# First batch's strided pairs: queries and keys as 2 KB rows, transposed by pairs of neighbouring tokens

## The chip, the cores and the metric

The kernel runs on one core of a Trainium2 chip. The metric is the device time of one execution in microseconds (us). Engines are named as in the profile: PE (TensorE) multiplies matrices, PEld is its weight load, DVE (VectorE), ACT (ScalarE) and POOL (GpSimd) work on vectors, SP (SyncE) issues transfers (DMAs). A few transfers of the start are issued by ACT.

## The reference

Attention over 8 batches, 8 heads, 576 tokens of 64 numbers, then a two-layer network over all 4608 tokens. The first four heads attend to the last 32 tokens ("local"), the last four to the earlier tokens whose number is the same modulo 32 ("strided").

```python
stride = 32
scores = scale * np.matmul(q, k.transpose(0, 1, 3, 2))
rel = pos[:, None] - pos[None, :]
mask_local = (rel >= 0) & (rel < stride)
mask_strided = (rel >= 0) & (pos[None, :] % stride == pos[:, None] % stride)
...
x = np.ascontiguousarray(attn_out.transpose(0, 2, 1, 3)).reshape(B * S, H * D)
h = x @ w_in            # 512 x 2048
g = h * np.clip(h + 3.0, 0.0, 6.0) / 6.0
return (g @ w_out).astype(np.float32)
```

The two weight matrices come as 64-bit floats. Queries, keys and values are 32-bit.

## The kernel before

**Heads by pairs.** Two heads of a batch, 2 x 64 rows, make a pair, four pairs a batch. In batch 0 pairs 0 and 1 are local, pairs 2 and 3 strided. `kept_pair(g)` lays out the work of one pair. For batch 0 (`early` is not 0):

- `load` (L488 to L491) brings queries (tile `qn`) and keys (`kn`) with eight successive tokens on each of 72 partitions. For each token and head this is a run of 64 numbers, 256 bytes, so one load has 72 x 8 x 2 = 1152 runs. It is issued as two DMAs, 64 partitions and 8.
- `tr` (L494 to L498) turns them by eight matmuls with the identity, one for each of the eight token places, into two PSUM banks (`qp`, `kp`): 128 rows (two heads of 64), 72 columns for each place. `evac` (L500 to L512) copies the banks into the layout that the scores read (`qplain`, `kplain`, and for strided pairs `qt`, `kt`).
- `scores` (L593 to L609) writes the mask by a matmul and adds queries by keys to it (`ps`, two banks). A local pair has 36 small matmuls, a strided one 64.
- Then the softmax: maximum and sum on DVE (`st`), subtraction and scaling on POOL (`e`, L636 to L668), exponential on ACT. Local pairs are turned back by PE (`turned`, `pt`, L725), strided ones by DVE (L702, L713, tiles `at`, `atkept`).
- `both` (L746) and `both_mm` (L766 to L772) multiply by the values (`pv`), and `keep_x` splits the result into a rounded part on ACT (L430) and a rest on DVE (L433): `x_00`, `x_01` for pair 0, up to `x_30`, `x_31`.

**Network.** `ffn(0)` multiplies these x tiles by the first weights (`ph`, L921 to L923: three matmuls for each chunk of 128 channels), in the order of `TURNS`: pair 0, 2, 1, 3. `gate_of` forms the gate on ACT (L956) and DVE (L960, tile `u`), then come the second weights (`acc`, L854 to L856).

**Weights.** `weight_part` loads each 128 x 512 block of 64-bit floats (`rawi`, `rawo`, L303, 512 KB) and turns it into two 32-bit tiles: two ACT passes, a DVE join (L319), a rounded part on ACT or POOL, a rest on POOL or DVE (L337).

**Order.** Nothing is issued in the order in which it is written. Each step is an `op` with an engine, a cost in us, the tiles that it reads and writes, and a due time. `Plan.emit` plays all steps through by these costs and writes the instructions of every engine in the order that comes out. A changed cost or due time can therefore move instructions everywhere in the program. `emit` also puts idle matmuls (`idle`, L1254) where it sees PE waiting early on. Each engine runs its own row in order, and waits at an instruction until its inputs are there.

Of the kernel before, what the change touches and what calls it, by code (L numbers as in the profile page):

```python
# [20 lines left out]
P = 128  # L21
# [4 lines left out]
NQB = 6  # L26
# [8 lines left out]
FIRST = (-57.0, -53.9, -56.5, -53.8)  # L35
QK = (-60.0, -59.0, -55.0, -52.0)
VAL = (-56.0, -53.0, -51.0, -49.0)
# [18 lines left out]
HOP = 0.12  # L56

WARM = 100.0
IDLE = 0.43
FETCH = 2.6  # L60
WORDS = 256
# [4 lines left out]
class Plan:  # L66
# [29 lines left out]
    def emit(self, idle):  # L96
# [6 lines left out]
        ready = {e: [] for o in ops for e in o[0]}  # L103
        free = dict.fromkeys(ready, 0.0)
        avail = [o[9] for o in ops]
# [81 lines left out]
def attention_ffn(ctx: ExitStack, tc, q, k, v, w_in, w_out, out):  # L187
# [252 lines left out]
    def kept_pair(g):  # L440
# [37 lines left out]
        for x in "qk":  # L478
# [6 lines left out]
            if early:  # L485

                def load(x=x, nkey=nkey):
                    t = new(wp, nkey, [P, RUN, 2, D], F32, f"{x}n{nm}")  # L488
                    rows = {"q": q, "k": k}[x][b, h0:h0 + 2].rearrange("j (p i) d -> p i j d", i=RUN)
                    for part in (slice(0, D), slice(D, S // RUN)):  # L490
                        (nc.scalar if g < 2 and x == "k" else nc.sync).dma_start(t[part], rows[part])  # L491
                tb = [slot(early) for _ in range(2)]

                def tr(x=x, nkey=nkey, tb=tb):  # L494
                    n = S // RUN
                    ps = [psum(tb[h], f"{x}p{nm}{h}") for h in range(2)]
                    for i in range(RUN):
                        nc.tensor.transpose(ps[i // 4][:, i % 4 * n:i % 4 * n + n], tiles[nkey][:n, i].rearrange("p j d -> p (j d)"), tiles["ident",][:n, :n])  # L498

                def evac(e, x=x, tb=tb, h=0):  # L500
                    ps, to, half = tiles[tb[h].key][:, :S // 2], qk_of(x), slice(RUN // 2 * h, RUN // 2 * h + RUN // 2)
                    if loc:
                        c0 = PAD if x == "k" else 0
                        to = to[:, c0:c0 + S].rearrange("c (p i) -> c p i", i=RUN)[:, :, half]
                        ps = ps.rearrange("c (i p) -> c p i", i=RUN // 2)
                    else:
                        to = to.rearrange("c (t a m) -> c t a m", t=RUN, a=4)[:, half, :, :NPOS]
                        ps = ps.rearrange("c (t m a) -> c t a m", t=RUN // 2, a=4)
                    if e == "ACT":
                        nc.scalar.copy(to, ps)  # L510
                    else:
                        nc.vector.tensor_copy(to, ps)  # L512
                op("ACT" if g < 2 and x == "k" else "SP", 1.7, load, writes=[nkey], due=QK[g] + 0.1 * (x == "k") - 900 * (g < 2 and x == "k"), after=1.7)
                op("PE", 0.7 * slow, tr, words=2 * RUN, reads=[("ident",), nkey, "plain", tkey[x]], writes=tb, take=tb, due=due - 1020, mode="s")
                for h in range(2):
                    op({"ACT": 0.45, "DVE": 0.4} if loc else {"ACT": 0.65, "DVE": 0.65}, 0, partial(evac, h=h), reads=[tb[h]],
                       writes=[tkey[x]] if h == 0 else [tkey[x] + (1,) if isinstance(tkey[x], tuple) else tkey[x] + "1"], give=tb[h], due=due - 19)
                continue
# [22 lines left out]
        def load_v():  # L541
# [14 lines left out]
            for a in range(4):  # L556
                nc.sync.dma_start(tiles[vkey][PAD * a:PAD * a + NPOS].rearrange("p j t d -> p j (t d)"), rows[a])
        op("SP", 3.9 if shifted else 1.5, load_v, writes=[vkey, skey] if shifted else [vkey], due=VAL[g] if early else due - 30, early=0 if early else due - 35, after=3.6 if shifted else 2.0)

# [54 lines left out]
        def keep(e, j):  # L614
# [8 lines left out]
        sd = due - 12  # L623
        op("PE", ((2.0 if loc else 1.75) if early else 1.5) * slow, scores, reads=["const", qkey, kkey, *both_halves], writes=[*sb, ekey, ekey + "1", stkey],
           take=sb, due=sd - 1000, room=0.0 if early else ROOM, mode="s", words=4 * 2 * (18 if loc else 32) + 6)
# [91 lines left out]
        if shifted:  # L717
# [16 lines left out]
            def both():  # L734
                ps, at, vt = [psum(vb[h], f"pv{nm}{h}") for h in range(2)], tiles[akey], tiles[vkey]
                half = 3 * NQB // 2
                for h in range(2):
                    for x in range(half):
                        for j in (h, 1 - h):
# [6 lines left out]
                            nc.tensor.matmul(ps[bank][own, PAD * x:PAD * x + PAD], vu, at[own, n0:n0 + PAD], start=True, stop=True)  # L746
            op("PE", 0.72 * slow, turned, reads=[("ident",), ekey, ekey + "1"], writes=[*tb, akey, akey + ("b",)], take=tb, due=due - 1002, mode="s", words=4 * NQB)
            for h in range(2):
# [16 lines left out]
        else:  # L765
            def both_mm():  # L766
                ps, vt = [psum(vb[h], f"pv{nm}{h}") for h in range(2)], tiles[vkey]
                for i in range(8):
                    for j in range(2):
                        at = tiles["at1", i // 4][:, i % 4] if akeys[j] == "at1" else tiles[akeys[j]][:, i]  # L770
                        nc.tensor.matmul(ps[i // 4][D * j:D * j + D, i % 4 * P:i % 4 * P + 4 * NPOS], vt[:, j, i],
                                         at.rearrange("p (a m) -> p a m", a=4)[:, :, :NPOS], start=True, stop=True)  # L772
# [515 lines left out]
```

## Time and profile before

| | |
|---|---|
| median of 3 runs | 928.04 us (926.23 to 931.61) |
| profiled execution | 929.12 us |
| its span, first to last instruction | 927.3 us |
| PE busy over the span | 885.3 us, 95% |
| DVE / ACT / POOL busy | 53% / 44% / 46% |
| mean granted PE clock | 0.978 |

The span is that of the profiled execution; its time is 1.8 us more. The busy shares are means over the whole program, in which attention of a batch and the network of others alternate, and say little of the first tenth, where batch 0 has to be loaded and attended before the network can start. The views by window and in order of time show that part by itself. In them a row has its start, its length, the engine and line, the tiles, and in brackets the idle time ahead of it with what ended it.

### The profile page before, as it was taken

How to read it: one execution, taken by the hardware profiler on the slowest of the kernel's cores; microseconds unless marked ns; L12 is line 12 of the kernel's file. 1: busy time of each engine (PE TensorE's matmuls, PEld its weight loads, DVE VectorE, ACT ScalarE, POOL GpSimd, SP SyncE). 2: the span in 40 equal slices, each digit the busy share in tenths (PEclk: the TensorE clock that was granted, in tenths of full speed). 3: DMA queues.
4: the chain of work that ended last, by engine and by line, in shares of the span. 5: the costliest groups of instructions: out<-in, count | busy, mean ns of one | idle time of the engine just before them, and what ended most of it. 6: DMA issues, size and time to landing. Idle time of an engine off the chain costs nothing.

```text
span 927.3 us, 19470 instructions
## 1 busy us (share of the span) xinstructions
PE 885.3 (95%) x7747; PEld 711.9 (77%) x7747; DVE 488.8 (53%) x833; ACT 404.6 (44%) x736; POOL 428.6 (46%) x378
## 2 busy tenths in 40 slices
PE   5789898999999999999999999999999999999997
PEld 3668686776888788888788778888887887888786
DVE  3788866568766777466755723345457003323200
ACT  2656655333434435344444633444446234334421
POOL 3646765555765877222221955213139531112441
PEclk7579999999999999999999999999999999999999
DMA  9988999977688874799784687785745675555374
GB/s 161 236 251 206 249 236 333 282 177 190 181 197 242 209 189 112 205 260 230 218 209 149 194 257 196 238 210 192 227 156 211 200 236 185 194 192 188 120 213 137
DMA packets 229563, 191.71 MB, mean 207 GB/s; under 512 B 174944, under 2 KB 189280, under 8 KB 229472
## 3 DMA queue, kind: packets, MB, share of 16 engines
q1 hardware_dynamic: 226800, 189.35, 73.2%
q10 hardware_dynamic: 2672, 1.11, 0.6%
q8 instruction: 61, 1.00, 0.5%
q14 instruction: 30, 0.25, 0.1%
HBM read 157.91 MB, written 32.51 MB: 205 GB/s over the span
## 4 chain that ended last, share of the span: by engine, by line
PE 75%; POOL 6%; DMA 6%; DVE 5%; SPq 3%; issue 2%; ACT 2%; DVEq 0%; POOLq 0%; ACTq 0%
PE ph L1094 8%; PE ph L1095 7%; PE ph L1096 7%; PE acc L854 4%; PE acc L856 4%; PE acc L855 4%; PE ph L921 3%; PE ph L922 3%; PE ph L923 3%; PE ps L608 3%; DMA rawi<-in_moe_w_in_dram 3%; DMA qn<-in_q_dram 2%; POOL xc L1033 2%; PE acc2b L854 2%; PE acc2b L856 2%
## 5 line engine op out<-in xcount | busy, mean ns | idle before, releaser
L1113 DVE TENSOR_TENSOR htmp<-ph,htmp 128x512 f32<-128x512 f32 x72 | 49.7, 690 | 183.9 <-ACT htmp L1105 106.7
L1094 PE MATMUL ph<-xc,wi 128*128 128x512 f32 x336 | 133.4, 397 | 1.3 <-DVE htmp L1113 0.8
L1095 PE MATMUL ph<-xc,wi 128*128 128x512 f32 x336 | 131.1, 390 | 0.0
L1096 PE MATMUL ph<-xc,wi 128*128 128x512 f32 x336 | 130.9, 390 | 0.0
L890 POOL TENSOR_TENSOR g<-u,g 128x512 fp32r<-128x512 f32 x48 | 65.7, 1372 | 62.1 <-ACT g L887 50.1
L921 PE MATMUL ph<-x,wi 128*128 128x512 f32 x192 | 79.8, 415 | 7.9 <-DVE u L960 4.6
L922 PE MATMUL ph<-x,wi 128*128 128x512 f32 x192 | 76.8, 400 | 4.0 <-DVE x L433 2.6
L923 PE MATMUL ph<-x,wi 128*128 128x512 f32 x192 | 76.7, 399 | 0.8 <-POOL wi L337 0.8
L854 PE MATMUL acc<-wo,g 128*128 128x512 f32 x192 | 76.9, 401 | 0.0
L855 PE MATMUL acc<-wo,g 128*128 128x512 f32 x192 | 75.1, 391 | 1.5 <-issue 1.1
L1094 PEld LDWEIGHTS ph<-xc,wi 128*128 128x128 f32 x336 | 63.0, 188 | 17.2 <-DVE htmp L1113 2.0
L856 PE MATMUL acc<-wo,g 128*128 128x512 f32 x192 | 75.4, 392 | 0.2 <-POOL g L890 0.2
L1096 PEld LDWEIGHTS ph<-xc,wi 128*128 128x128 f32 x336 | 63.1, 188 | 13.4
L1095 PEld LDWEIGHTS ph<-xc,wi 128*128 128x128 f32 x336 | 63.1, 188 | 12.4
L708 DVE STREAM_TRANSPOSE atloc<-e 32x192 f32<-32x192 f32 x168 | 61.9, 369 | 15.9 <-POOL e L668 9.0
L1105 ACT COPY htmp<-ph 128x512 f32<-128x512 f32 x72 | 42.2, 587 | 50.0 <-PE ph L1096 48.1
L653 POOL TENSOR_TENSOR e<-e,st 128x288 f32<-128x288 f32 (+1 forms) x30 | 34.2, 1141 | 64.5 <-DVE st L631 64.4
L890 POOL TENSOR_TENSOR g12a<-u,g02a 128x512 fp32r<-128x512 f32 x16 | 20.6, 1289 | 83.4 <-ACT g02a L887 83.4
L956 ACT ACTIVATE u<-htmp,three 128x512 f32<-128x512 f32 x48 | 34.7, 723 | 44.5 <-DVE htmp L1113 44.5
L956 ACT ACTIVATE u<-ph,three 128x512 f32<-128x512 f32 x48 | 33.0, 688 | 44.2 <-PE ph L923 43.8
L960 DVE SCALAR_TENSOR_TENSOR u<-u,htmp 128x512 f32<-128x512 f32 x48 | 38.5, 802 | 22.9 <-ACT u L956 22.8
L890 POOL TENSOR_TENSOR g11a<-u,g01a 128x512 fp32r<-128x512 f32 x16 | 21.5, 1347 | 60.4 <-ACT g01a L887 52.2
(212 smaller groups left out, 2079.5 us busy)
## 6 DMA issues: line engine op xcount, KB each, us to landing
wo<-wod SPq DMA_DIRECT2D x128, 512.0 KB
wi<-wid SPq DMA_DIRECT2D x84, 512.0 KB
rawi<-in_moe_w_in_dram SPq DMA_DIRECT2D x16, 512.0 KB
rawo<-in_moe_w_out_dram SPq DMA_DIRECT2D x16, 512.0 KB
wod<-wo SPq DMA_DIRECT2D x16, 512.0 KB
wid<-st SPq DMA_DIRECT2D x64, 128.0 KB
qn<-in_q_dram SPq DMA_DIRECT2D x112, 72.0 KB
kn<-in_k_dram SPq DMA_DIRECT2D x112, 72.0 KB
```

Of the source, the lines that this page charges most:

```text
L708: nc.vector.transpose(at[PAD * (a + h):PAD * (a + h) + PAD, :, PAD * a:PAD * a + PAD], e[PAD * a:PAD * a + PAD, :, PAD * h:PAD * h + PAD])
L854: nc.tensor.matmul(acc, gh, woh, start=fc == 0, stop=False)
L855: nc.tensor.matmul(acc, gh, wol, start=False, stop=False)
L856: nc.tensor.matmul(acc, gl, woh, start=False, stop=end)
L890: on(e).tensor_tensor(out=to(1), in0=tiles[uk], in1=tiles[gk[0]].bitcast(F32), op=ALU.subtract)
L921: nc.tensor.matmul(ph, wih, xh, start=n_ == 0, stop=False)
L922: nc.tensor.matmul(ph, wih, xl, start=False, stop=False)
L923: nc.tensor.matmul(ph, wil, xh, start=False, stop=n_ == NCC - 1)
L956: nc.scalar.activation(make(), src(), AF.Relu, bias=three)
L1094: nc.tensor.matmul(ph, w[:, j, 0], x[:, 0], start=u in (0, 1, 3) and j == 0, stop=False, skip_group_check=u in (2, 4, 5, 6))
L1095: nc.tensor.matmul(ph, w[:, j, 0], x[:, 1], start=False, stop=False, skip_group_check=u in (2, 4, 5, 6))
L1096: nc.tensor.matmul(ph, w[:, j, 1], x[:, 0], start=False, stop=j == 1, skip_group_check=u in (2, 4, 5, 6))
```

## The change

For the strided pairs of batch 0 the load now keeps the eight tokens of a partition together: 512 numbers, 2 KB, for each of two heads, so 72 x 2 = 144 runs, issued as one DMA of 72 partitions. A matmul of `tr` now takes 128 numbers of one head, two neighbouring tokens, and its 128 result rows are (token parity, 64 numbers) where they were (head, 64 numbers). Banks and blocks of scores are divided by parity where they were divided by head. `both_mm` follows: the block's number and the bank index change places, and the matmuls come in another order (`ORDER`). The number of matmuls is the same in each step. The local pairs keep their loads.

Beside it the planner's table is new: `QK` (when queries and keys are due, strided pairs earlier), `SIDE` (which loads ACT issues, the same two as before), `FETCH`, `BEGIN`, and the costs of several steps.

```diff
-QK = (-60.0, -59.0, -55.0, -52.0)
+QK = (-60.0, -59.0, -58.0, -57.0)
+SIDE = ("k", "k", "", "")
...
+ORDER = [(u + 4 * h, j) for u in range(4) for j in range(2) for h in range(2)]
-FETCH = 2.6
+FETCH = 2.2
+BEGIN = 0.75
...
-        free = dict.fromkeys(ready, 0.0)
+        free = dict.fromkeys(ready, BEGIN)
...
                 def load(x=x, nkey=nkey):
+                    if not loc:
+                        t = new(wp, nkey, [P, 2, RUN * D], F32, f"{x}n{nm}")
+                        rows = {"q": q, "k": k}[x][b, h0:h0 + 2].rearrange("j (p i) d -> p j (i d)", i=RUN)
+                        (nc.scalar if x in SIDE[g] else nc.sync).dma_start(t[:S // RUN], rows)
+                        return
                     t = new(wp, nkey, [P, RUN, 2, D], F32, f"{x}n{nm}")
...
                     for i in range(RUN):
-                        nc.tensor.transpose(ps[i // 4][:, i % 4 * n:i % 4 * n + n], tiles[nkey][:n, i].rearrange("p j d -> p (j d)"), tiles["ident",][:n, :n])
+                        own = tiles[nkey][:n, i].rearrange("p j d -> p (j d)") if loc else tiles[nkey][:n, i // 4, i % 4 * P:i % 4 * P + P]
+                        nc.tensor.transpose(ps[i // 4][:, i % 4 * n:i % 4 * n + n], own, tiles["ident",][:n, :n])
...
-                op("ACT" if g < 2 and x == "k" else "SP", 1.7, load, writes=[nkey], due=QK[g] + 0.1 * (x == "k") - 900 * (g < 2 and x == "k"), after=1.7)
+                op("ACT" if x in SIDE[g] else "SP", 1.8 if loc else 0.75, load, writes=[nkey], due=QK[g] + 0.1 * (x == "k") - 900 * (x in SIDE[g]), after=1.95 if loc else 1.3)
...
-        op("PE", ((2.0 if loc else 1.75) if early else 1.5) * slow, scores, reads=["const", qkey, kkey, *both_halves], writes=[*sb, ekey, ekey + "1", stkey],
+        op("PE", (1.45 if loc else 1.1) * slow if early else 1.5, scores, reads=["const", qkey, kkey, *both_halves], writes=[*sb, ekey, ekey + "1", stkey],
...
-                for i in range(8):
-                    for j in range(2):
+                for i, j in ORDER if early else [(i, j) for i in range(8) for j in range(2)]:
                         at = tiles["at1", i // 4][:, i % 4] if akeys[j] == "at1" else tiles[akeys[j]][:, i]
-                        nc.tensor.matmul(ps[i // 4][D * j:D * j + D, i % 4 * P:i % 4 * P + 4 * NPOS], vt[:, j, i],
+                        h, t = (i // 4, i % 4 * 2 + j) if early else (j, i)
+                        nc.tensor.matmul(ps[t // 4][D * h:D * h + D, t % 4 * P:t % 4 * P + 4 * NPOS], vt[:, h, t],
```

Three places show what the planner makes of it. The first is SP's row of transfers near the start, behind the first load `qn_0`. `qn_1` is the query load of pair 1, `v_0` and `vlast` the values of pair 0, `rawi` a block of weights. Before:

```order
L491 DMA qn_2_155<-in_q_dram 64x16x64
L491 DMA qn_2_155<-in_q_dram 8x16x64
L549 DMA v_0_171<-in_v_dram 64x16x64
L550 DMA vlast<-in_v_dram 64x64
L549 DMA v_0_171<-in_v_dram 64x16x64
L550 DMA vlast<-in_v_dram 64x64
L303 DMA rawi_210<-in_moe_w_in_dram 128x1024
L303 DMA rawi_215<-in_moe_w_in_dram 128x1024
L491 DMA qn_1_227<-in_q_dram 64x16x64
L491 DMA qn_1_227<-in_q_dram 8x16x64
L491 DMA kn_1_274<-in_k_dram 64x16x64
L491 DMA kn_1_274<-in_k_dram 8x16x64
```

Now:

```order
L494 DMA qn_2_156<-in_q_dram 72x2x512
L499 DMA qn_1_163<-in_q_dram 64x16x64
L499 DMA qn_1_163<-in_q_dram 8x16x64
L499 DMA kn_1_190<-in_k_dram 64x16x64
L499 DMA kn_1_190<-in_k_dram 8x16x64
L494 DMA qn_3_198<-in_q_dram 72x2x512
L306 DMA rawi_210<-in_moe_w_in_dram 128x1024
L494 DMA kn_3_212<-in_k_dram 72x2x512
L306 DMA rawi_226<-in_moe_w_in_dram 128x1024
L558 DMA v_0_228<-in_v_dram 64x16x64
```

All queries and keys now stand ahead of the values of pair 0, which were third; those of pair 3 have moved from behind the fourth block of weights to around the first.

The second place is PE's row around the scores of pair 2 (`ps_20`, `ps_21`). Before, the scores came first and the transposes of pair 1 behind them:

```order
L608 MATMUL ps_20_311<-kplain,qt_2_163 32x18
L608 MATMUL ps_21_312<-kplain,qt_2_163 32x18
L498 MATMUL qp_10_395<-ident,qn_1_227 128x72 x4
L498 MATMUL qp_11_396<-ident,qn_1_227 128x72 x4
L498 MATMUL kp_10_424<-ident,kn_1_274 128x72 x4
L498 MATMUL kp_11_425<-ident,kn_1_274 128x72 x4
L725 MATMUL pt_00_447<-ident,e 128x96 x3
L725 MATMUL pt_01_448<-ident,e 128x96 x3
```

Now the transposes of pair 1 stand directly behind those of pair 2's keys, and the scores follow, from their masks on:

```order
L507 MATMUL kp_20_278<-ident,kn_2_158 128x72 x4
L507 MATMUL kp_21_279<-ident,kn_2_158 128x72 x4
L507 MATMUL qp_10_300<-ident,qn_1_163 128x72 x4
L507 MATMUL qp_11_301<-ident,qn_1_163 128x72 x4
L507 MATMUL kp_10_315<-ident,kn_1_190 128x72 x4
L507 MATMUL kp_11_316<-ident,kn_1_190 128x72 x4
L606 LDWEIGHTS eye
L606 MATMUL ps_20_335<-mtri,eye 128x144
```

The scores of pair 2 have moved behind 16 matmuls that need `qn_1` and `kn_1`. Further on, the transposes of pair 3 have moved in the same way ahead of the scores of pair 1, seven idle matmuls stand ahead of `pv_2`, and nine products of pair 0 (`ph_0`, `ph_1`, `ph_2`) stand ahead of the turning of pair 1 (`pt_1`), where six stood.

The third place is DVE's row at the end of batch 0's attention, up to the second half of `x_31`, the last input of the first products. Before:

```order
L433 TENSOR_TENSOR x_11_875<-pv_11_811,x_10_874 128x224
L319 SCALAR_TENSOR_TENSOR fo_854<-fo_854,rawo_506 128x512
L319 SCALAR_TENSOR_TENSOR fi_862<-fi_862,rawi_511 128x512
L319 SCALAR_TENSOR_TENSOR fi_905<-fi_905,rawi_514 128x512
L433 TENSOR_TENSOR x_31_941<-pv_30_911,x_30_940 128x4x4x16
L319 SCALAR_TENSOR_TENSOR fi_931<-fi_931,rawi_520 128x512
L337 TENSOR_TENSOR wi_944<-fi_862,wi_944 128x4x128
L433 TENSOR_TENSOR x_31_941<-pv_31_912,x_30_940 128x4x4x16
```

Now:

```order
L436 TENSOR_TENSOR x_11_879<-pv_11_807,x_10_878 128x224
L322 SCALAR_TENSOR_TENSOR fo_850<-fo_850,rawo_448 128x512
L322 SCALAR_TENSOR_TENSOR fo_858<-fo_858,rawo_451 128x512
L436 TENSOR_TENSOR x_31_925<-pv_30_896,x_30_924 128x4x4x16
L322 SCALAR_TENSOR_TENSOR fi_887<-fi_887,rawi_464 128x512
L340 TENSOR_TENSOR wo_938<-fo_858,wo_938 128x512
L436 TENSOR_TENSOR x_31_925<-pv_31_897,x_30_924 128x4x4x16
```

Between the copy `at_1` (the turned scores of pair 1, further up) and this point stand four joins where six stood; two have moved behind the first gates.

More of the change, by code (lines that the diff above doesn't have):

```diff
@@ L490, in load @@
                     for part in (slice(0, D), slice(D, S // RUN)):
-                        (nc.scalar if g < 2 and x == "k" else nc.sync).dma_start(t[part], rows[part])
+                        (nc.scalar if x in SIDE[g] else nc.sync).dma_start(t[part], rows[part])
                 tb = [slot(early) for _ in range(2)]
@@ L512, in evac @@
                         nc.vector.tensor_copy(to, ps)
-                op("ACT" if g < 2 and x == "k" else "SP", 1.7, load, writes=[nkey], due=QK[g] + 0.1 * (x == "k") - 900 * (g < 2 and x == "k"), after=1.7)
+                op("ACT" if x in SIDE[g] else "SP", 1.8 if loc else 0.75, load, writes=[nkey], due=QK[g] + 0.1 * (x == "k") - 900 * (x in SIDE[g]), after=1.95 if loc else 1.3)
                 op("PE", 0.7 * slow, tr, words=2 * RUN, reads=[("ident",), nkey, "plain", tkey[x]], writes=tb, take=tb, due=due - 1020, mode="s")
                 for h in range(2):
-                    op({"ACT": 0.45, "DVE": 0.4} if loc else {"ACT": 0.65, "DVE": 0.65}, 0, partial(evac, h=h), reads=[tb[h]],
+                    op({"ACT": 0.41, "DVE": 0.46}, 0, partial(evac, h=h), reads=[tb[h]],
                        writes=[tkey[x]] if h == 0 else [tkey[x] + (1,) if isinstance(tkey[x], tuple) else tkey[x] + "1"], give=tb[h], due=due - 19)
@@ L557, in load_v @@
                 nc.sync.dma_start(tiles[vkey][PAD * a:PAD * a + NPOS].rearrange("p j t d -> p j (t d)"), rows[a])
-        op("SP", 3.9 if shifted else 1.5, load_v, writes=[vkey, skey] if shifted else [vkey], due=VAL[g] if early else due - 30, early=0 if early else due - 35, after=3.6 if shifted else 2.0)
+        op("SP", 3.0 if shifted else 1.5, load_v, writes=[vkey, skey] if shifted else [vkey], due=VAL[g] if early else due - 30, early=0 if early else due - 35, after=3.7 if shifted else 1.5 if early else 2.0)
         ekey = "el" if loc else "es"
@@ L746, in both @@
                             nc.tensor.matmul(ps[bank][own, PAD * x:PAD * x + PAD], vu, at[own, n0:n0 + PAD], start=True, stop=True)
-            op("PE", 0.72 * slow, turned, reads=[("ident",), ekey, ekey + "1"], writes=[*tb, akey, akey + ("b",)], take=tb, due=due - 1002, mode="s", words=4 * NQB)
+            op("PE", 0.69 * slow, turned, reads=[("ident",), ekey, ekey + "1"], writes=[*tb, akey, akey + ("b",)], take=tb, due=due - 1002, mode="s", words=4 * NQB)
             for h in range(2):
```

## The prediction

> **What bounds the kernel now.** I read the page's slices first (40 slices of 23.2 us; PE is the busy share of PE in tenths, PEclk its granted clock), then the busy times by window, then PE's waits and its row in order of time.
>
> ```profile
> PE   5789898999999999999999999999999999999997
> PEclk7579999999999999999999999999999999999999
> DMA  9988999977688874799784687785745675555374
> ```
>
> ```profile
> core 0: us, PE busy (x) PEld busy (x) DVE busy (x) ACT busy (x) POOL busy (x), PEclk, DMA share, GB/s
> 0.00:13.00 13.00, 6.54 (x31) 3.30 (x32) 5.37 (x10) 2.08 (x3) 5.62 (x28) 0.83 1.09 125
> 13.00:24.00 11.00, 6.74 (x202) 4.75 (x205) 3.88 (x9) 2.87 (x6) 3.22 (x4) 0.66 1.15 208
> 24.00:46.00 22.00, 16.94 (x382) 14.88 (x382) 17.68 (x40) 14.46 (x33) 15.02 (x16) 0.58 1.04 234
> 46.00:53.00 7.00, 7.00 (x90) 5.82 (x90) 3.96 (x9) 4.43 (x9) 2.46 (x3) 0.76 1.03 408
> 53.00:64.00 11.00, 7.85 (x58) 5.70 (x57) 10.87 (x21) 5.90 (x14) 8.22 (x9) 0.96 0.86 148
> 64.00:100.00 36.00, 36.00 (x413) 28.85 (x413) 27.84 (x42) 22.43 (x43) 19.79 (x17) 0.92 0.87 232
> 100.00:155.00 55.00, 48.88 (x460) 38.10 (x458) 41.51 (x73) 31.78 (x57) 35.93 (x28) 1.00 0.96 278
> 155.00:320.00 165.00, 160.37 (x1890) 127.18 (x1891) 114.40 (x206) 69.25 (x135) 105.94 (x98) 1.00 0.82 210
> 320.00:927.00 607.00, 594.97 (x4240) 483.27 (x4238) 263.31 (x426) 251.36 (x440) 232.42 (x179) 1.00 0.67 197
> ```
>
> From 64 us on PE is the bound (840 of 863 us busy), and almost all its work is untouched, so what matters is when that stretch begins. Up to 53 us the transfer engines are full (share above 1) while the rate is half of the 408 GB/s that weight blocks alone reach. PE runs at about half clock there and waits:
>
> ```profile
> PE qp L498 <- DMA qn<-in_q_dram: 5.2, 3, 2.5
> PE ps L608 <- issue: 4.3, 1, 4.3
> PE ph L921 <- POOL e L653: 3.2, 1, 3.2
> PE ph L922 <- DVE x L433: 2.6, 1, 2.6
> ```
>
> ```profile
> 7.97 0.72 PE L498 MATMUL qp<-ident,qn 72*128 72x72 f32 x8 [2.27 <-DMA qn<-in_q_dram]
> 12.55 1.19 PE L498 MATMUL qp<-ident,qn 72*128 72x72 f32 x8 [2.47 <-DMA qn<-in_q_dram]
> 18.65 1.02 PE L608 MATMUL ps<-kplain,qt 64*32 64x18 f32 x97
> 23.94 0.45 PE L608 MATMUL ps<-kplain,qt 64*32 64x18 f32 x31 [4.26 <-issue]
> 31.81 1.19 PE L498 MATMUL qp<-ident,qn 72*128 72x72 f32 x8 [0.46 <-DMA qn<-in_q_dram]
> 38.49 0.38 PE L771 MATMUL pv<-atkept,v 128*64 128x72 f32 x1
> 40.96 1.46 PE L608 MATMUL ps<-kt,qt 64*32 64x18 f32 x128
> 45.59 0.40 PE L921 MATMUL ph<-x,wi 128*128 128x512 f32 x1 [3.17 <-POOL e L653]
> 47.76 1.16 PE L725 MATMUL pt<-ident,e 96*128 96x96 f32 x6
> 63.90 0.80 PE L922 MATMUL ph<-x,wi 128*128 128x512 f32 x1 [2.63 <-DVE x L433]
> ```
>
> Two of these stops are no wait for data. At 19.67 PE stops in the middle of the 128 score matmuls of pair 2, all of whose inputs are there, and POOL's L653, named at 45.59, is not an input of L921. Four rows explain them: PE's code comes by transfer.
>
> ```profile
> PE 885.3 (95%) x7747; PEld 711.9 (77%) x7747; DVE 488.8 (53%) x833; ACT 404.6 (44%) x736; POOL 428.6 (46%) x378
> q8 instruction: 61, 1.00, 0.5%
> 0.00:19.67 19.67, 13.21 (x221) 8.00 (x222) 8.43 (x17) 4.56 (x9) 7.23 (x30) 0.74 1.11 156
> 0.00:42.45 42.45, 29.81 (x601) 22.39 (x602) 24.62 (x56) 17.67 (x38) 21.31 (x45) 0.64 1.09 181
> ```
>
> 15,494 instructions over 61 packets of queue 8 are 254 a packet. PE stops after 443 and after 1203 instructions, 760 apart, three packets. So I read both stops as code that arrives late on full transfer engines: 4.27 us, then 3.14 us.
>
> **The change part by part.**
>
> *Transfers.* Two windows price them:
>
> ```profile
> DMA packets 16378, 11.93 MB, mean 234 GB/s; under 512 B 14188, under 2 KB 14188, under 8 KB 16371
> DMA packets 780, 2.86 MB, mean 408 GB/s; under 512 B 85, under 2 KB 85, under 8 KB 779
> ```
>
> The first is 2 to 53 us, the second 46 to 53. In the first, 16 blocks of 512 KB (8.4 MB) and two strided value loads (0.59 MB) take 22 us at 408 GB/s. The other 29 us carry eight query and key loads of 1152 runs and 4352 runs of local values: 2.14 ns a run, 120 GB/s. One load of 295 KB therefore costs 2.46 us now. With 2 KB rows its price lies between 0.72 us (408 GB/s) and 2.46 us. A line through the engine time of a run, 34 ns for 256 B (16 x 2.14) and 160 ns for 4 KB, gives 93 ns for 2 KB, and 144 x 93 / 16 = 0.84 us; I take that, as the 4 KB row is the nearer one. Four loads: 6.5 us less engine time (bounds 0 and 7.0), so the last early weight block lands near 47 us. The rows of PE stay: eight matmuls in each `tr`, 64 in the scores, 16 in `both_mm`, at the same sizes; evacuation copies the same 288 columns. These edits cost nothing, and `ORDER` neither, as adjacent matmuls still go to two halves.
>
> The Trainium skill ("DMA: Bandwidth & Descriptors", section "Why a DMA increments its semaphore by 16 and not by 1") states that a transfer from SP or ACT uses the largest number of engines up to 16 that divides its outer dimension: 12 for 72 rows, 16 for the 64 rows of before. By it a load would cost 0.84 x 16 / 12 = 1.1 us, an estimate, and the forecast would be some 0.3 us later, as one such load lies on the first chain. No row of this run separates the engines.
>
> *Start.* `qn_0` and `kn_0` are as before (7.97). Behind them `qn_2` and `kn_2` come in 2 x 0.84 us where they took 2 x 2.46, shared with values: near 10.0 where it was 12.55 (bounds 9.7, when PE is done with pair 0, and 12.55). Gain 2.5. With 1.19 for `qp_2`, 2.5 for the scores of pair 0 and 1.2 for `kp_2`, PE is ready for pair 1 near 15. `qn_1` and `kn_1`, 2.46 us each behind that, land near 12 and 14.5, so this new wait is covered by 0.5 to 3 us. Then 2.3 us of transposes and the scores of pair 2 from 17.
>
> *First code stop.* The 443rd instruction now falls in the last third of these scores, near 18.3. Packet 3 was asked for somewhere in the scores of pair 0 and came at 23.94. Those scores are 2.4 us earlier, and fewer short rows stand ahead: 18.3 (no stop) to 21.5; I take a stop of 1 us. The scores end near 20 against 24.4: 4.4 us gained (2.9 to 5.5).
>
> *Pair 2 to 3.* From the end of its scores to `pv_2` pair 2 took 14.1 us (24.4 to 38.49), part of it PE's transposes of pair 3, the `pv_0` of 4 us and keys ahead of it. Now the transposes of pair 3 (2.4), `pt_0` (1.2) and the scores of pair 1 (2.5) come first, `pv_0` at 26 to 30. `v_0` has moved behind: by the prices above it lands near 24, cover 2 us. Seven idle matmuls of 0.43 fill up to 33, when DVE's transposes for pair 2 end too. `pv_2` at 33: 5.5 gained. The second code stop stays, since 1203 falls at the end of the scores of pair 3 again: first products near 39.8. Three more of them at 0.43 stand ahead of `pt_1`: 4.5 to 5 gained there.
>
> *Last input.* From 49 to 64 DVE does not rest (10.87 of 11 us above). What ends it:
>
> ```profile
> 57.69 1.70 DVE L319 SCALAR_TENSOR_TENSOR fi<-fi,rawi 128x512 int32<-128x512 int32 x2
> 59.86 1.80 DVE L319 SCALAR_TENSOR_TENSOR fi<-fi,rawi 128x512 int32<-128x512 int32 x1
> 61.59 1.75 DVE L337 TENSOR_TENSOR wi<-fi,wi 128x512 fp32r<-128x512 f32 x1
> 63.26 0.58 DVE L433 TENSOR_TENSOR x<-pv,x 128x256 fp32r<-128x256 f32 x1
> ```
>
> Two joins fewer stand ahead of `x_31`: 0.85 to 1.8 each, so 1.7 to 3.6; I count only 1, since the rest of the stretch also waits for PE's `pv_3`. `x_31` ends near 58.3 instead of 63.84: 5.5 gained.
>
> *Given back.* The two joins run behind the first gates. DVE has 8 us free in 64 to 100, but in 64 to 320 PE already waits for it:
>
> ```profile
> PE ph L921 <- DVE u L960: 4.6, 4, 2.2
> ```
>
> Bounds: 0, and 3.6 if all of it shows. I take 0.9. Reordering of the later rows I price at 0: the products are the same, and 320 to 927 has 12 us of idle time in all.
>
> *Sum.* 929.12 - 5.5 + 0.9 = 924.5 for the profiled execution; it lies 1.1 above the median, so 923.4 on the median's scale, a gain of 4.6 us.
>
> **Rivals.**
>
> *Given back in full.* The start is early, but the conversions of weights (three DVE, ACT and POOL passes a block) do not keep pace in 100 to 155, where transfers are at 0.96 and DVE at 75%. For it: the four waits above. Against: the blocks land 6 us earlier too. 2.6 of 5.5 lost: 925 to 926.5, say 926.
>
> *The shorter loads are hidden.* The code stops and DVE's backlog keep the start near 63: the change does what it says and nothing shows. For it: only 5.2 us of PE's waits name a load. Against: the code is late because of the transfers. 928.
>
> *Both code stops vanish.* With 6.5 us of transfer time gone, code arrives in time: 3 us more, 920. Against: the second stop has weight blocks beside it, which stay.
>
> *Slower: `kn_1` holds the scores of pair 2.* SP issues in order, and its second half of `kn_1` stood for 4.5 us before:
>
> ```profile
> 14.27 5.19 SPq L491 DMA_DIRECT2D kn<-in_k_dram  x2
> ```
>
> Now all of PE's row is behind it: if `kn_1` lands at 17 or earlier nothing is lost; each us later moves everything behind. Landing as before (transposed at 25.3) would put the end of pair 2's scores at 25.3 + 1.2 + 1.9 = 28.4 against 24.4, 4 us later: 932. Against: `kn_1` stands sixth on SP now, with no values or weights ahead.
>
> **How the numbers follow.** Forecast 0.60 (its own range 921.5 to 925), given back 0.14, hidden 0.08, no stops 0.08, slower 0.10. About 0.5%, 4.6 us, is what a measurement of this kernel tells from no change. The forecast lies on that bound; the changes that I counted low (joins, stop) make me give two thirds of it to faster: 0.40 + 0.08 = 0.48. Same: 0.20 + 0.14 + 0.08 = 0.42. Slower 0.10. The range 918.5 to 928.6 leaves out the slower case and little else.
>
> **What would show it.** Right: `qp_2` near 10, pair 2's scores done by 21, `pv_2` near 33, `x_31` done near 58, the full 408 GB/s phase over by 48, PE's idle time behind 64 us not above 24. Wrong: `qp_1` or `kp_1` waiting for its load, a code stop of 4 us at pair 2, `pv_0` waiting for `v_0`, or more waits of `ph` for `u`.

## The result, and the profile after

| | before | after |
|---|---|---|
| median of 14 runs each | 928.06 us | 934.33 us (930.68 to 936.64) |
| ratio, with its 95% interval | | 1.0051 (1.0033 to 1.0069) |
| profiled execution | 929.12 us | 931.56 us |
| PE busy over the span | 885.3 us | 888.0 us |

The change makes the kernel slower by half a per cent. The forecast was 923.4 us, 4.6 us faster, and the range ended at 928.6. The profiled execution of the changed kernel is one of its faster ones, 2.8 us under its median, while that of the kernel before is 1.1 us over its own. A second profiled execution of the changed kernel, taken later, stood at 938.52 us; what follows is of the first unless it is said otherwise.

The busy times of the changed kernel by window, in the columns used before:

```profile
core 0: us, PE busy (x) PEld busy (x) DVE busy (x) ACT busy (x) POOL busy (x), PEclk, DMA share, GB/s
0.00:13.00 13.00, 6.90 (x30) 3.74 (x31) 5.37 (x10) 2.08 (x3) 5.62 (x28) 0.82 0.86 120
13.00:24.00 11.00, 7.29 (x192) 6.12 (x191) 4.24 (x10) 3.26 (x8) 3.23 (x4) 0.50 1.09 183
24.00:46.00 22.00, 19.05 (x389) 15.02 (x389) 17.49 (x40) 12.49 (x27) 12.31 (x15) 0.58 0.97 220
46.00:53.00 7.00, 7.00 (x90) 5.79 (x89) 3.83 (x12) 4.65 (x10) 1.96 (x3) 0.77 1.03 408
53.00:64.00 11.00, 8.79 (x61) 6.36 (x60) 9.40 (x19) 6.58 (x13) 6.77 (x7) 0.95 0.82 187
64.00:100.00 36.00, 35.95 (x489) 28.59 (x488) 32.38 (x47) 25.06 (x48) 25.34 (x23) 0.97 0.91 240
100.00:155.00 55.00, 50.97 (x402) 40.14 (x401) 40.72 (x71) 31.28 (x56) 35.91 (x29) 1.00 0.96 293
155.00:320.00 165.00, 156.64 (x1872) 123.43 (x1871) 110.64 (x199) 67.82 (x135) 110.91 (x99) 1.00 0.83 206
320.00:929.00 609.00, 595.42 (x4236) 482.33 (x4234) 261.06 (x426) 249.07 (x438) 232.98 (x181) 1.00 0.66 196
```

Three things are to be seen. The first 13 us move no more bytes than before (120 GB/s against 125), although the engines' share is down from 1.09 to 0.86: the time that the engines gained was not filled. The 408 GB/s phase is still in the window from 46 to 53. And the stretch from 155 to 320, in which no step's work was changed, holds 8.4 us in which PE is idle (165 less 156.64), where it held 4.6.

PE's waits up to 64 us, and its rows there in order of time:

```profile
PE ps L617 <- issue: 6.7, 2, 4.5
PE qp L507 <- DMA qn<-in_q_dram: 4.0, 2, 2.8
PE ph L930 <- ACT x L433: 1.1, 1, 1.1
PE ph L931 <- DVE x L436: 1.1, 1, 1.1
```

```profile
10.08 1.19 PE L507 MATMUL kp<-ident,kn 72*128 72x72 f32 x8 [0.36 <-DMA kn<-in_k_dram]
12.49 1.20 PE L507 MATMUL qp<-ident,qn 72*128 72x72 f32 x8 [1.22 <-DMA qn<-in_q_dram]
24.80 0.67 PE L617 MATMUL ps<-kplain,qt 64*32 64x18 f32 x44 [4.52 <-issue]
34.76 3.17 PE L1263 MATMUL idle<-eye 128*128 128x512 bf16 x7
43.14 0.24 PE L617 MATMUL ps<-kt,qt 64*32 64x18 f32 x2 [2.14 <-issue]
61.73 0.50 PE L931 MATMUL ph<-x,wi 128*128 128x512 f32 x1 [1.06 <-DVE x L436]
```

`qp_2` (12.49) comes no earlier than it did (12.55), and the first code stop is as long as it was. The scores of pair 2 end at 25.47, 1.1 us later than before (24.39). Still, the last input of the network's first products is there at 61.73, against 63.90, a gain of 2.2 us. It belongs to the order of the start: over the profiles of this study PE goes on there at 63.9 to 66.0 in the four with the old start, and in the nine with the new one at 56.2 to 61.9 eight times and once at 64.4.

The stops that the view calls "issue" are code that arrives late, as the prediction read them. The trace records the packets of queue 8, which carries instructions, with their times, us:

| first stop | PE stops | packet starts | packet ends | PE goes on |
|---|---|---|---|---|
| before | 19.68 | 20.75 | 22.30 | 23.94 |
| after | 20.29 | 21.93 | 23.20 | 24.80 |

In the 14 profiles of this study there are 72 such stops of over 0.4 us (the start of the program left out), and 71 of them end 1.2 to 2.0 us behind the end of a packet of queue 8.

The 2.2 us are lost behind. PE's waits from 155 to 420 us, first of the changed kernel, then of the kernel before:

```profile
PE ph L930 <- DVE u L969: 4.4, 6, 1.1
PE ps L617 <- issue: 3.5, 3, 2.2
PE acc L863 <- issue: 2.1, 2, 1.7
```

```profile
PE ps L597 <- DVE x L433: 1.4, 1, 1.4
PE acc L855 <- issue: 1.1, 1, 1.1
PE ph L921 <- DVE u L960: 1.0, 2, 0.8
PE ps L608 <- issue: 0.8, 1, 0.8
```

Waits of `ph` for the gate `u` went from 1.0 to 4.4 us, and code stops ("issue") from 1.9 to 5.6. Taken from PE's row, all stops of over 0.4 us between 150 and 420 us sum to 4.5 us before and 9.5 after.

What makes a gate late can be read from DVE's and POOL's rows at the wait that ends at 358.30. After:

```profile
354.31 3.13 DVE L672 TENSOR_TENSOR st<-st,eps 96x12 f32<-96x12 f32 x1
357.47 0.22 DVE L673 RECIPROCAL st<-st 96x12 f32<-96x12 f32 x1
357.62 0.62 DVE L969 SCALAR_TENSOR_TENSOR u<-u,ph 128x512 f32<-128x512 f32 x1
356.13 1.28 POOL L1048 TENSOR_TENSOR hxf<-hxf,hxf 128x512 f32<-128x512 f32 x1
```

Before:

```profile
352.88 0.98 DVE L663 TENSOR_TENSOR st<-st,eps 96x12 f32<-96x12 f32 x1
356.05 0.69 DVE L960 SCALAR_TENSOR_TENSOR u<-u,ph 128x512 f32<-128x512 f32 x1 [1.94 <-ACT u L956]
```

ACT had its part of the gate done at 355.29, but DVE came to it at 357.62 only: ahead of it in DVE's row stands a small step of the softmax, which took 3.13 us. It ends 0.03 us behind a pass of POOL (357.41), and POOL had run without a pause. Over all profiles this step takes 0.16 to 0.18 us in the 235 cases in which POOL is idle, and up to 3.13 us in the 213 others, of which 187 end within 0.06 us of a POOL pass. In all seven profiles with the changed kernel's order behind 180 us the same three gates are late in this way, ahead of matmuls 2560, 2768 and 3923 of PE's row (idle ones not counted), for 2.7 to 3.2 us together; in the kernel before and the four others with its order there, PE has no stop of over 0.4 us at any of the three.

To see when it is lost, I laid the rows of PE over each other by work: each matmul (idle ones left out) counts with the usual distance to the next of its kind, and the lead of a kernel at a time is how much earlier than the kernel before it had done the same sum. One profiled execution each, us, minus is behind:

| at | 70 | 100 | 140 | 180 | 240 | 260 | 360 | 500 |
|---|---|---|---|---|---|---|---|---|
| after | 3.4 | 2.9 | 3.0 | 5.0 | 3.2 | 0.7 | -1.3 | -2.0 |

A lead of 5.0 us at 180 becomes a debt of 1.3 at 360. In the later execution of 938.52 us the lead of 3.2 at 70 was a debt of 1.2 at 110 already, 2.0 at 180, and 8.4 at 360.

### The profile page after: what moved, and what is told of

It is laid out like the page before. It is cut to its first block, busy times and chain, and to the rows that moved or that the text cites. A ratio compares the mean times of both kernels' runs of the same rounds, so it can differ in the third digit from the quotient of the medians.

```text
span 929.7 us, 19504 instructions
## 1 busy us (share of the span) xinstructions
PE 888.0 (96%) x7749; PEld 711.5 (77%) x7749; DVE 485.1 (52%) x829; ACT 402.3 (43%) x732; POOL 435.0 (47%) x386
## 4 chain that ended last, share of the span: by engine, by line
PE 75%; DVE 6%; DMA 6%; POOL 6%; issue 3%; ACT 2%; SPq 2%; DVEq 0%; POOLq 0%; ACTq 0%
PE ph L1103 8%; PE ph L1104 7%; PE ph L1105 7%; PE acc L863 4%; PE ph L930 4%; PE acc L865 3%; PE acc L864 3%; PE ph L931 3%; PE ph L932 3%; PE ps L617 3%; PE pv L405 2%; DMA kn<-in_k_dram 2%; DMA rawi<-in_moe_w_in_dram 2%; POOL xc L1042 2%; PE acc2b L863 2%
## 5 line engine op out<-in xcount | busy, mean ns | idle before, releaser
L717 DVE STREAM_TRANSPOSE atloc<-e 32x192 f32<-32x192 f32 x168 | 61.9, 368 | 13.2 <-POOL e L677 5.8
L930 PEld LDWEIGHTS ph<-x,wi 128*128 128x128 f32 x192 | 36.9, 192 | 22.1 <-DVE u L969 12.4
```

The lines of the kernel that those rows point to most:

```text
L717: nc.vector.transpose(at[PAD * (a + h):PAD * (a + h) + PAD, :, PAD * a:PAD * a + PAD], e[PAD * a:PAD * a + PAD, :, PAD * h:PAD * h + PAD])
L930: nc.tensor.matmul(ph, wih, xh, start=n_ == 0, stop=False)
```

## The experiments

Kernels that were measured together share a chip and its runs of the kernel before; ratios are to those.

### Loads or table

The change has two parts: loads and products (2 KB rows, pairs of tokens, `ORDER`), and the planner's table (`QK`, `FETCH`, `BEGIN`, costs). The first kernel is the changed one with the whole old table set back, these numbers and the costs of the steps:

```diff
-QK = (-60.0, -59.0, -58.0, -57.0)
+QK = (-60.0, -59.0, -55.0, -52.0)
...
-FETCH = 2.2
-BEGIN = 0.75
+FETCH = 2.6
+BEGIN = 0.0
```

> The 2 KB loads, the transposes by token pairs and the new order of the value products, with the whole planner table of before, so that every engine's row is that of before except for one load DMA in place of two. Theory A (the loss comes from the order that the new table writes for the rest of the program, behind 175 us, where the change was still 4.4 us ahead in the trace): not slower than before, -2 to +1 us. Theory B (the new loads or products themselves cost the time): +4 to +7 us.

The second has the old loads and products, and the new table:

```diff
+QK = (-60.0, -59.0, -58.0, -57.0)
-QK = (-60.0, -59.0, -55.0, -52.0)
...
-FETCH = 2.6
+FETCH = 2.2
+BEGIN = 0.75
```

> The loads, transposes and products of before, with the new planner table, so that the order is that of the change. Theory A: the order of the rest loses 7 to 10 us and the start gains less without the shorter loads: +4 to +10 us. Theory B: within 2 us of before.

Rows only: 929.67 us, 0.9990 (0.9974 to 1.0006) of before, which stood at 930.5 beside them. Table only: 931.56, 1.0017 (1.0001 to 1.0034). So in the old order the new loads and products cost nothing that shows, and they bring nothing. The new table alone costs 1.1 us, which is not the 4 to 10 of theory A and within the 2 us of theory B. The two do not add up to the changed kernel's 1.0051: most of its loss needs both, the new table and the new loads. A part of that is found below, when the loads are cut in two. With the table alone `qp_2` started at 12.49, on loads in 256 B runs: the very time of the changed kernel with its 2 KB rows.

### Start or rest

The planner was made to plan twice, with the new and with the old table, and to take the order of one up to a planned time and that of the other behind it. All four kernels have the change's loads and products.

```diff
+HEAD, CUT = "new", 66.0
...
+        new, old = self.plan(self.ops, 2.2, 0.75), self.plan(self.olds, 2.6, 0.0)
+        head, tail = (new, old) if HEAD == "new" else (old, new)
+        rows = [(n, e, head[1]) for t, _, n, e in head[0] if t < CUT]
+        done = {n for n, _, _ in rows}
+        rows += [(n, e, tail[1]) for t, _, n, e in tail[0] if (t >= CUT if n is None else n not in done)]
```

> The change, with the order of the new table for the steps that it plans up to 66 us (batch 0 and the first products) and the order of the old table for all steps behind. Theory A: the start gain stays and the loss is gone, -3 to -5 us. Theory B: +4 to +7 us as in the change.

> The new loads with the order of the old table up to 66 planned us, and the order of the new table behind. Theory A: +5 to +10 us. Theory B: as the run with the rows alone, +4 to +7 us; if the rows cost nothing and the start's order is what loses, 0.

> The changed kernel, in the new table's order for all steps planned up to 180 us and in the old table's order behind. At equal work the changed kernel was 5 us ahead of the one before at 180 us and lost 8 us between 180 and 240. Theory A (the loss is the new order between 180 and 400 us): with the old order there the lead of 5 at 180 stays, in part at least; 924 to 927 where before is 929.5, ratio 0.994 to 0.997. Theory B (the old order's rest is held by things with times of their own, weights that land or gates, as at 130 to 155 us, and gives any lead back): lead at 240 us under 1, end within 0.8 of before. Theory C (the new start leaves debts, work put off, that have to be paid behind 180 whatever the order): 930.5 or more.

> The counterpart: the change's loads and products, in the old table's order for steps planned up to 180 us, in the new table's order behind. Theory A: no lead at 180 us (0.5 at most, as with the old order throughout), then the new order's loss of 180 to 240 us, 5 to 8, of which it recovers 3 to 5 later as in the changed kernel it did not; 932 to 936. Theory B and C: the loss of 180 to 240 was the lead handed back or the debts paid, and neither is there now; within 1 of before, 928.5 to 930.5.

| order up to the cut, cut, order behind | us | ratio (95%) | lead at 70 | at 180 | at 360 |
|---|---|---|---|---|---|
| new, 66, old | 929.30 | 0.9992 (0.9978 to 1.0006) | 5.4 | 0.0 | 0.6 |
| old, 66, new | 932.68 | 1.0023 (1.0009 to 1.0038) | 0.4 | 3.7 | -2.6 |
| new, 180, old | 927.42 | 0.9971 (0.9955 to 0.9987) | 6.9 | 1.7 | 1.1 |
| old, 180, new | 937.11 | 1.0060 (1.0037 to 1.0083) | -0.8 | -2.7 | -7.3 |

Wherever the new order stands behind 180 us, the kernel falls back by 4.6 to 6.3 us between 180 and 360 (3.7 to -2.6, -2.7 to -7.3, in the changed kernel 5.0 to -1.3), also when there was no lead to hand back and no work put off. With the old order behind 180 the lead changes by 0.6 at most. That is the loss that theory A names, and it rules out B and C of the two runs that cut at 180. The times expected were met less well. The two kernels that cut at 66 lie 1.2 us under and 2.2 us over the one before, where A had said 3 to 5 under and 5 to 10 over: of the first the lead was gone by 140 us, the second gained 3.7 by 180 that I had not counted. And the third reached 0.9971 at the edge of A's range, but with a lead of 1.7 at 180 where A had counted on 5. It is faster than the kernel before and the changed one by measurement, 3.4 us under the one before (930.81 beside it), which is less than the half per cent by which the forecast counted.

Its waits of PE from 155 to 420 show what is gone; the code stops of 3.5 at `ps` are not there, and `u` is waited for half as long:

```profile
PE ph L956 <- DVE u L995: 2.1, 3, 1.6
PE ps L632 <- DVE x L460: 1.4, 1, 1.4
PE acc L889 <- issue: 1.0, 1, 1.0
```

These runs show a second loss, which I had expected to be smaller. A lead of 5.4 at 70 us in the first of them is 2.7 at 130 and 0.1 at 140; in the third 6.9 at 70 is gone at 110. The last step of the first can be followed. ACT's and DVE's rows in order of time, first of that kernel:

```profile
130.14 0.67 ACT L338 ACTIVATE fi<-rawi 128x512 f32<-128x512 f32 x1 [4.54 <-DMA rawi<-in_moe_w_in_dram]
131.58 0.69 DVE L346 SCALAR_TENSOR_TENSOR fi<-fi,rawi 128x512 int32<-128x512 int32 x1 [5.38 <-ACT rawi L342]
132.19 0.68 DVE L995 SCALAR_TENSOR_TENSOR u<-u,ph 128x512 f32<-128x512 f32 x1
```

and of the kernel before:

```profile
130.04 0.68 ACT L311 ACTIVATE fi<-rawi 128x512 f32<-128x512 f32 x1 [1.79 <-DMA rawi<-in_moe_w_in_dram]
131.51 0.69 DVE L319 SCALAR_TENSOR_TENSOR fi<-fi,rawi 128x512 int32<-128x512 int32 x1 [2.65 <-ACT rawi L315]
132.12 0.68 DVE L960 SCALAR_TENSOR_TENSOR u<-u,ph 128x512 f32<-128x512 f32 x1
```

A block of weights lands at 130.1 in both, whatever the engines had gained by then. The kernel that is 2.75 us ahead waits 2.75 us longer for it (4.54 against 1.79), DVE stands at the join `fi`, and the gate `u` that PE needs is behind the join in DVE's row. SP had issued that block 1.1 us earlier (121.8 against 122.9), but the transfer engines are full there (share 1.02 from 120 to 130 in both). So these 2.7 us end at the transfer; what took as much between 70 and 130 is not followed here.

### Is it the price of a code fetch, or any other order

`FETCH` is what the planner takes a code fetch of PE to cost. It went from 2.6 to 2.2, and it acts on the whole program. One kernel sets it back; the other moves it by 0.01, which means nothing, but gives another order: 990 of the 5652 rows of PE's order stand elsewhere, all behind row 1771.

```diff
 e9
-FETCH = 2.2
+FETCH = 2.6
 e10
-FETCH = 2.2
+FETCH = 2.21
```

> The changed kernel with one number of the planner set back, FETCH 2.6 instead of 2.2 (the planned price of a code fetch), and the whole order planned again; no instruction's work is changed. It moves 2298 of PE's 5652 rows, from the first row on. In the changed kernel PE's stops of over 0.4 us between 150 and 420 us sum to 9.6 us, in the kernel before to 5.6. Theory P (the lower price itself packs the code fetches and gates worse): stops of 3 to 6 us there, 0.996 to 1.001 of before. Theory D (any change of a price draws another order, and the changed kernel's was a bad draw): the stops are at other places and sum to anything from 3 to 10; 0.995 to 1.006.

> The changed kernel with FETCH 2.21 instead of 2.2: a price without meaning, which still moves 990 of PE's 5652 rows, all behind row 1771. Theory D: the stops behind 150 us move, and the time leaves the changed kernel's 1.0051 by 0.002 or more in either direction. Theory P: the price is what decides, stops of 8 to 10 us again, 1.0035 to 1.0067.

2.6 gave 931.51 us, 1.0026 (1.0007 to 1.0044). 2.21 gave 937.83 us in six runs, 1.0099 (1.0071 to 1.0127), by the ratios some 4.5 us above the changed kernel, on another chip. The stops of over 0.4 us between 150 and 420 us sum to 6.7 and 10.6 us. With 2.21 five of the ten stand at the very matmuls of the changed kernel (1857, 2111, 2228, 2492, 2560), 6.1 us of the 10.6, and the other five elsewhere: the stops moved only in part. (The 5.6 us that the expectation gives for the kernel before are 4.5 when counted in the same way.) In the last kernel, from 155 to 420:

```profile
PE ph L930 <- DVE u L969: 5.1, 6, 1.7
PE acc L863 <- issue: 1.7, 1, 1.7
PE ps L617 <- issue: 1.7, 3, 1.0
PE acc L863 <- ACT g L896: 1.5, 1, 1.5
PE pv L405 <- DVE atloc L717: 0.8, 1, 0.8
```

Both times lie outside theory P's ranges and, for 2.21, the difference is of theory D's size: a step of no meaning in the price moved the time by as much as the whole change did. Each new table draws a new order for the 700 us that nobody edited, and the kernels seen here lie between 0.997 and 1.010. What makes a draw bad is seen only in its signs, gates that come late by about 1 us each, behind a DVE step that waits out POOL, and code that stops PE at a place where nothing else can run.

### Why the 2 KB loads were not earlier

Before, a load went out as two DMAs, 64 partitions and 8; the changed one is a single DMA of 72. This kernel cuts it again and leaves all else:

```diff
-                        (nc.scalar if x in SIDE[g] else nc.sync).dma_start(t[:S // RUN], rows)
+                        for part in (slice(0, D), slice(D, S // RUN)):
+                            (nc.scalar if x in SIDE[g] else nc.sync).dma_start(t[part], rows[part])
```

> The changed kernel, with the strided loads of 72 partitions issued as two DMAs again, 64 partitions and 8, still of 2 KB runs. Order otherwise the same. In the changed kernel kp_0 ran at 10.08 (8.50 before), qp_2 at 12.49 (12.55 before), and the mean share of the DMA engines was 0.95 to 1.09 from 6 to 12 us where it was 1.41 before, with work queued all the time. Theory: one DMA of 72 partitions occupies fewer of the 16 engines than one of 64, so that the shorter transfer is not an earlier one; then here the share returns to 1.3 or more, kp_0 to 8.5 to 9, and qp_2 comes at 10.0 to 11.3. Rival: the landing is set by what shares the engines (the local loads of 256 B runs and the other queue), whichever way the load is cut; then qp_2 stays within 0.4 of 12.49. Time: the start does not reach the end by either theory if the order behind decides, so 932 to 935.

931.19 us, 1.0006 (0.9983 to 1.0029). The transfers between 6 and 12 us, of the kernel before, the changed one and this one, are one line each:

```profile
DMA packets 3171, 0.80 MB, mean 133 GB/s; under 512 B 3171, under 2 KB 3171, under 8 KB 3171
```

```profile
DMA packets 1339, 0.80 MB, mean 133 GB/s; under 512 B 1079, under 2 KB 1079, under 8 KB 1339
```

```profile
DMA packets 2309, 1.02 MB, mean 170 GB/s; under 512 B 2057, under 2 KB 2057, under 8 KB 2309
```

The changed kernel needs less than half of the packets and moves the same 0.80 MB: the long rows lower the mean share of the engines from 1.41 to 1.02 without being done sooner, though transfers are queued all the time. Cut in two, the same rows move 1.02 MB at a share of 1.14 (1.3 or more was expected). And `kp_0` and `qp_2` come earlier:

```profile
9.67 1.17 PE L508 MATMUL kp<-ident,kn 72*128 72x72 f32 x8
11.13 1.19 PE L508 MATMUL qp<-ident,qn 72*128 72x72 f32 x8 [0.29 <-DMA qn<-in_q_dram]
```

For `qp_2` that is the first theory (10.0 to 11.3 expected); `kp_0` went less than half of the way (8.5 to 9 expected). PE's granted clock was 1.00 in this profile from 8 to 40 us, where the changed kernel had 0.50 to 0.60; the last kernel below has `qp_2` at 11.28 with a clock of 0.50 from 8 to 20 us, so the earlier load does not hang on it. The time came out lower than either theory said, so I ran both kernels again side by side.

> The changed kernel itself once more, on the same chip as the run split_again, so that the two can be compared without a second chip between them. 1.0033 to 1.0069 of before, as first measured.

> The changed kernel with the strided loads cut into 64 and 8 partitions, once more, beside the changed kernel. Theory S (the cut load brings the start 1.4 us forward, and the new order carries a lead to 180 us, so that it reaches the end): 2 to 5 us below the changed kernel of this call, 0.995 to 0.998 of it. Theory N (the 4 us between the two were the chips and the scatter; a lead of the start is handed back, as in the runs with the old order behind): within 0.0015 of the changed kernel.

Changed kernel 934.10 us, 1.0041 (1.0023 to 1.0059); cut loads 931.19, 1.0014 (0.9993 to 1.0035). The second to the first, from the twelve times of each, is 0.9967 (0.9950 to 0.9985): some 3 us from cutting four DMAs. With its loads cut the changed kernel, 1.0006 and 1.0014, is not told from the kernel before, and it agrees with the new table on the old loads (1.0017). `qp_2` stood at 12.32 and 11.87 in their profiles. Between 64 and 155 us PE waited for `u` 8.0 us in the one and 1.5 in the other:

```profile
PE ph L930 <- DVE u L969: 8.0, 3, 3.9
```

```profile
PE ph L931 <- DVE u L970: 1.5, 1, 1.5
```

The wait of 3.9 ends at 109 us; ahead of its gate DVE's row has a transpose of the next queries, which waits 2.1 us for their load. The first profile of the changed kernel waited 4.0 us for `u` in that stretch. So theory S has the right time, but its path is not what this profile shows: here the cut kernel had the last input of the first products later than the other (64.39 against 61.91, behind a second code stop of 4.69 us) and the smaller lead at 70 us (2.3 against 3.2). At 180 it led by 4.9, the other was 2.0 behind. Where the 3 us come from is open; these two executions are 7.9 us apart, nearly all of it won between 70 and 180 us, where the waits for the gate are.

The last kernel joins both: new order up to 180, old behind, and cut loads.

> The new table's order up to 180 planned us, the old table's behind (the kernel of the run new_to_180), and the strided loads cut into 64 and 8 partitions as in the run split_load. new_to_180 stood at 0.9971 of before, the cut load brought the changed kernel from 1.0051 to 1.0006. Theory: the two gains lie at different places (the first 20 us; behind 180) and add: 0.993 to 0.996, 924 to 927.5 where before is 930.8. Rival: what the start gains is handed back at 100 to 155 us, where in new_to_180 a lead of 6.8 fell to nothing while a gate waited; then within 0.0015 of that run, 0.9956 to 0.9986.

926.27 us, 0.9966 (0.9950 to 0.9982). The gains do not add, as the rival said, though the interval reaches into the theory's range too. Its lead of 7.0 at 70 us is still 3.2 at 130, and at 180 it is 1.5, as without the cut. It is 3 to 4 us faster than the kernel before, and with the kernel of the same order without the cut the best that I found.

## Why the prediction was wrong

**The step that failed** is this one: "Reordering of the later rows I price at 0: the products are the same, and 320 to 927 has 12 us of idle time in all." Not the products but the gates and the code fetches between them decide, and the limit that I set on the loss looked at the wrong stretch and from the wrong side: the idle time of the old order says nothing of what a new order can add. It is 4.6 to 6.3 us between 180 and 360, whatever stood ahead, and enough to turn a gain into a loss: with the old order behind 180 the same loads stand at 0.9971 and not at 1.0051.

The sum shows its weight. It gave 924.5 for a profiled execution that stood at 931.56, 7.0 us more. At 70 us the lead was 3.4 where 5.5 were counted, 2.1 short; from there to the end 5.8 went (3.4 ahead to 2.4 behind) where 0.9 were counted, 4.9 more. The median is 3.9 us further from the forecast, as the one profiled execution lies 2.8 us under its median and the other 1.1 over.

**Transfers.** "Four loads: 6.5 us less engine time" was too much, and it took for granted that freed engines are filled. The price of 93 ns for a 2 KB row was drawn between 256 B and 4 KB rows, though the kernel before has 2 KB rows in its strided values: between 24 and 46 us 288 of their packets took 148 ns each. In the changed kernel the packets of `qn_2` and `kn_2` took 214 ns and those of `qn_3` and `kn_3` 173, which is 1.9 and 1.6 us a load over 16 engines and not 0.84: some 2.9 us less for the four. The page of the Trainium skill that the prediction weighed ("DMA: Bandwidth & Descriptors", section "Why a DMA increments its semaphore by 16 and not by 1") gives 12 engines for 72 rows by its rule. By that rule I had added 0.3 us and kept it out of the sum. The runs agree with its direction: `qp_2` came at 11.8 to 12.5 in the five profiles with this start and the load in one DMA, at 11.1 to 11.9 in the three with the load cut. No row separates the engines.

**Start.** `qp_2` "near 10.0": 12.49, 0.06 us gained where 2.5 was counted. `qn_1` and `kn_1` were in time, as said, so the slower rival (`kn_1` holds the scores) did not occur.

**First code stop.** The place was right: in every profile of this study it stands behind matmul 220 or 221 with their weight loads, 441 or 443 instructions (predicted 443), and the second behind 1203 or 1204. The length was wrong: 4.52 us, not 1, and pair 2's scores ended at 25.47 where 20 was said. The forecast made it depend on how early and how free the transfers are; over the 14 profiles it was 1.5 to 4.5 us. The packet that ends it takes 1.3 to 1.8 us and PE goes on 1.4 to 1.8 us behind it, so the length is set by when the packet starts, 18.6 to 22.2 us; in 13 of the 14 that is only after PE has stopped. What starts it, and whether it was asked for in the scores of pair 0, no row shows.

**Pair 2 to 3, and the last input.** The seven idle matmuls came, but from 34.76 and not up to 33, and `pv_2` at 37.86 gained 0.6 us of 5.5. The second stop stayed, as said, at the end of pair 3's scores; it was 1.0 us shorter (2.14 against 3.17), and the first products came at 43.31 (39.8 forecast, 45.59 before). `x_31` was to be done at 58.3; it ends at 61.68, 2.2 us gained of 5.5.

**Given back** was 0.9, with 3.6 as its upper bound. The new start with the old order behind 66 gave back all of 5.4, and a bound was the wrong form for it: a lead that meets a transfer with a time of its own is worth nothing there, however large. The rival "given back in full" (0.14) was itself priced at 2.6 of 5.5 only. It named the conversions of weights at 100 to 155; the place is right for the last 2.7 us, and what holds there is the landing of the block ahead of them.

**What was to show it wrong** did: more waits of `ph` for `u` (4.0 against 3.6 us from 64 to 155, 4.4 against 1.0 from 155 to 420), a code stop of 4 us, and 26.0 us of PE idle time behind 64 us (865 less 839.0 busy) where 24 was the limit.

## What to carry to other kernels

A kernel whose order comes from a planner's table is drawn anew as a whole when a number in the table changes. So price the reordering by a run with a change of no meaning in the table, here 0.5% of the time, before crediting or blaming an edit; or fix the order behind the edited stretch, as the cut at 180 us did. A lead gained at the start is worth what is left of it at the first thing with a time of its own behind it, here a weight block on full transfer engines. And count bytes a window, not packets or engine share, to see whether a transfer became faster.

## What the runs showed of the hardware

- Between 6 and 12 us, beside other loads, kernels with 2 KB rows in one DMA of 72 partitions moved 0.80 MB (changed), 0.78 (changed, again) and 0.86 (rows only); with 256 B runs in DMAs of 64 and 8 it was 0.80 (before) and 0.88 (table only), with 2 KB rows in 64 and 8 it was 1.02, 0.97 and 1.00.
- PE's code comes in packets of 16,384 bytes on queue 8, 61 in the kernel before. With full transfer engines at the start PE stood still for 1.5 to 4.5 us, until 1.4 to 1.8 us behind the first of them; 71 of 72 stops that the profile calls "issue" end 1.2 to 2.0 us behind such a packet.
- A DVE step of 96 x 12 or 128 x 16 numbers with two inputs (`st`, L672) took 0.16 to 0.18 us with POOL idle and up to 3.13 us beside POOL's passes, ending with one in 187 of 213 cases.
- With the table alone, PE's granted clock was 1.00 in all windows from 8 to 40 us, where the kernel before had 0.50 to 0.72; that execution led by 10.5 us at 70 us, and by 2.8 at 110. I had not expected so large a lead to vanish in 40 us. The clock was 1.00 there in two more profiles, with the loads cut (927.39 us) and with `FETCH` 2.6 (935.02 us), so a full clock at the start does not make a fast execution. Leads of single executions at 70 us carry this difference with them. Why the clock differed is open.
- Of two executions of the changed kernel, 931.56 and 938.52 us, the second had 4 us more of waits for the gate between 64 and 155 us (8.0 against 4.0), with the same code; at the longest of them DVE had waited 2.1 us for a load.
